# Two of four weight sums added by VectorE into buffers of their own, and row numbers with a buffer per expert

## The chip, the cores and the metric

One core of a Trainium2 chip runs the whole program. The metric is the time of one execution on the device, in microseconds.

## The reference

Attention over 8 batches, 8 heads, 576 tokens and 64 columns a head, each token looking back over 128 tokens with a linear bias; its result is 4608 rows of 512 columns. Each row then goes to one of eight experts:

```
expert_idx = argmax(xn @ en.T / tau, axis=1)      # one expert for each row
for e in range(8):
    mask = expert_idx == e
    h = np.maximum(x[mask] @ w1[e], 0.0)          # w1[e]: 512 x 1024
    out[mask] = gate_w[mask, None] * (h @ w2[e])  # w2[e]: 1024 x 512
```

## The kernel before

Attention takes the first 260 us or so, and its last steps sort the rows by expert into a table in HBM, each with its row number and its gate. Then come the experts, one after the other, in the order of `TURNS` (a list of ranks, the fullest expert being rank 0, of which attention has already done a part). Every value is kept as a pair of fp16 tiles, a high and a low part, and a product is three matmuls. For each expert there is a hidden layer (`x @ w1`, TensorE, with the ReLU and the splitting into two parts done by ScalarE and VectorE) and an output layer (`h @ w2`, in tiles of 128 rows, each 24 matmuls of 512 columns; ScalarE scales the result by the gate, GpSimd stores the rows with an indirect DMA by their numbers).

**The hidden layer with seven products.** The first two experts use a plain product. For the six others (`PLAIN = 2`) `w1` is cut into four quarters of 256 x 512 and the rows of `x` into halves, and seven products stand for eight. The seven weights are three quarters, named `11`, `21` and `22`, and four sums: `t1` and `t3`, each of two quarters, `t2`, which is `t3` and one quarter more, and `t4`, which is `t2` and another one. In the list `SEVEN` the products follow in the order `11`, `t2`, `t3`, `t1`, `21`, `t4`, `22`, four times over (`ft`), and write the banks `ps7a` to `ps7d`. Between them `combine` (lines 1540 on) works: ScalarE copies `ps7a` to `s` (line 1546), VectorE adds it to `ps7b` and that to `ps7d` (both `u`, line 1543), and `ps7b` is then rewritten from `ps7c` and `u` (line 1544), which the last product into `ps7c` needs.

**The weights of the sums.** `fetch_quarter` (line 1417) loads a quarter of fp32 by SyncE's queue; five are loaded. `gather` (line 1421) lets an accumulating DMA of GpSimd's queue add another quarter onto a tile that has landed (line 1425). `t1` and `t3` are made so. For `t2` and `t4` the tile of `t3` is used again: once it has been split, a DMA adds a quarter onto it, that is split as `t2`, a DMA adds another one, and that is split as `t4`. `split` (line 1427) makes the fp16 pair: ScalarE the high part (line 1437), VectorE the low part (line 1435). The pair's tile holds all seven weights and there is one (`w1s=1`), so no split of an expert runs before the seven products of the expert ahead of it are done: the splits lie in that expert's output layer. `fetch` and `part` do the same for `w2` (lines 1409, 1489 and 1487), whose tiles of fp32 come from the same pool of `WSTG = 8` buffers as the quarters.

**Row numbers.** `row_info` (line 1380) is VectorE's: it converts `info`, the loaded numbers and gates of an expert (line 1395), compares the places with the count (1396), writes the row numbers `ids` (1397) and the gates `gs` (1398). It runs for the next expert while the current one starts. `ids` and `gs` have two buffers each. `put` stores a tile of 128 rows to the places in `ids`.

**The order of the work.** `Plan` is a scheduler in the kernel's own text. Each job has an engine, an estimated time, jobs it comes after, buffers it takes (`makes`) and uses, and a due time; for loads also an estimate of the landing (`land`) and of the time on the shared DMA path (`moves`). It lays the jobs out in time by these estimates, picks by due time, lets `fill` jobs give way to others that become ready soon, and emits them; every engine then runs its own list in that order, and waits at each instruction until its inputs are there. `row_info` is planned after the stores of the expert two turns back (`rows=2`), with no landing time for a store.

Of the kernel before, what the change touches and what calls it, by code (L numbers as in the profile page):

```python
# [15 lines left out]
F32 = mybir.dt.float32  # L16
I32 = mybir.dt.int32
AF = mybir.ActivationFunctionType
ALU = mybir.AluOpType
# [4 lines left out]
P = 128  # L24
# [16 lines left out]
GUARD = 32  # L41
PLAIN = 2
XSUM = "DVE"
PIECES = {
    "11": (0, (0, 0), 1),
    "22": (2, (1, 1), 1),
    "21": (1, (1, 0), 1),
    "t3": (5, (1, 1), 1),
    "t1": (3, (0, 1), -1),
}  # L50
CHAINS = {"t1": [(0, 0)], "t3": [(0, 1)], "t2": [(0, 0)], "t4": [(1, 0)]}
WIDTHS = {"t2": (4, -1), "t4": (6, 1)}
SEVEN = [
    ("a", 0, ("x", 0, 0)),
    ("b", 4, ("s", 2, 0)),
# [13 lines left out]
ORDER = -1e9  # L69
# [139 lines left out]
def kernel(  # L209
# [11 lines left out]
    nc = tc.nc  # L221
    B, H, S, D = q.shape
    NTOK, DM = out.shape
    E, _, F = moe_w1.shape
# [1085 lines left out]
    def moe(mctx):  # L1310
        def pool(nm, n):
            return mctx.enter_context(tc.tile_pool(name=nm, bufs=n))

        xt, yp, st, ht, wT, wS, zp = (
            pool(*a)
            for a in (("xt", 2), ("yp", 3), ("wstage", WSTG), ("ht", 1), ("wthird", 1), ("wseven", 1), ("xsum", 1))
        )
        MB = (MAXCAP + P - 1) // P
        MH = max(SLOTS[s] for s in TURNS[PLAIN:]) // 2
        HF = F // 2  # L1320
# [58 lines left out]

        def row_info(s):  # L1380
            (nb, hb), b0, info = blocks(s), first_row(s) // P, state[s]["info"]
            ids = yp.tile([P, MB], I32, tag="ids", name=f"ids_{s}", bufs=2)
            gs = yp.tile([P, MB], F32, tag="gs", name=f"gs_{s}", bufs=2)
            jobs = [(slice(0, P), slice(b0, nb), ids[:, b0:nb], gs[:, b0:nb])]
            if hb:
                pr, pk = tail_rows(s), packs.setdefault(PACKED[s][0], {})
                if not pk:
                    pk["ids"] = yp.tile([P, 1], I32, tag="ids2", name=f"ids2_{s}", bufs=2)
                    pk["gs"] = yp.tile([P, 1], F32, tag="gs2", name=f"gs2_{s}", bufs=2)
                jobs.append((pr, slice(nb, nb + 1), pk["ids"][pr], pk["gs"][pr]))  # L1390
# [23 lines left out]
        def quarter_of(s, q, e):  # L1414
            return moe_w1[ds(e, 1), q[0] * DM // 2 : (q[0] + 1) * DM // 2, q[1] * HF : (q[1] + 1) * HF].rearrange("o (c p) f -> p (o c) f", p=P)

        def fetch_quarter(s, what):
            ws[s, what] = x = st.tile([P, 2, HF], F32, tag="ws", name=f"ws_{what}_{s}")
            nc.sync.dma_start(x, quarter_of(s, PIECES[what][1], state[s]["e"]))

        def gather(s, what, q):

            if what in ("t2", "t4"):
                ws[s, what] = ws[s, "t3"]
            nc.gpsimd.dma_start(ws[s, what], quarter_of(s, q, state[s]["ep"]), accum_op=ALU.add)  # L1425

        def split(s, what, lo):

            if "w1" not in state[s]:
                state[s]["w1"] = [wS.tile([P, 7, 2, HF], F16, tag=f"w1{n}", name=f"w1{n}_{s}") for n in "hl"]  # L1430
            at, sign = WIDTHS[what] if what in WIDTHS else PIECES[what][::2]
            x = ws[s, what].rearrange("p a f -> p (a f)")
            hi, lo_ = (a[:, at].rearrange("p a f -> p (a f)") for a in state[s]["w1"])
            if lo:
                nc.vector.scalar_tensor_tensor(lo_, x, sign * SW, hi, op0=ALU.mult, op1=ALU.subtract)  # L1435
            else:
                nc.scalar.activation(hi, x, AF.Copy, scale=sign * SW)  # L1437
# [200 lines left out]
        def before(name):  # L1638
            return [(name, ORDER)]
# [6 lines left out]
            pe_last = name  # L1646

        starts = {}
        t = 0.0
        for p, s in enumerate(TURNS):  # L1650
            starts[s] = t
# [3 lines left out]
        for p, s in enumerate(TURNS):  # L1655
# [17 lines left out]
            if p:  # L1673
                last_ = TURNS[p - 1]
                m = starts[last_] + 24 * (0.42 * SLOTS[last_] + 5) * (3.5 if p > PLAIN else 4 if p > 1 else 2)
                sp_last = None
                seven_ = p >= PLAIN
                first_gets = [("q", what) for what in ("t3", "t1", "22", "21", "11")] if seven_ else [(1, c) for c in range(4)]
                for n, (w_, c) in enumerate(first_gets + [(2, c) for c in range(4)]):
                    d = (lead - 3000 if w_ != 2 else m) + 1500 * n  # L1680
                    if w_ == "q":
                        name, key, emit = f"getq_{s}_{c}", ("ws", s, c), lambda a=(s, c): fetch_quarter(*a)
                    else:
                        name, key, emit = f"get{w_}_{s}_{c}", ("ws", p, s, w_, c), lambda a=(p, s, w_, c): fetch(*a)
                    J(
                        name, "SP", 640, emit, land=1800, moves=1400, makes=[("ws", key)], due=d,
                        after=before(f"expert{s}") + before(f"rows{last_}") + (before(sp_last) if sp_last else []),
                    )
                    sp_last = name
                if seven_:  # L1690
                    J(f"epool{s}", "POOL", 600, lambda s=s: expert_on_pool(s), after=[f"expert{s}"], due=lead - 2000)
                    wt = {"t2": "t3", "t4": "t3"}
                    dep = {"t1": "getq_{}_t1", "t3": "getq_{}_t3", "t2": "slo_{}_t3", "t4": "slo_{}_t2"}
                    for what in ("t3", "t1", "t2", "t4"):
                        q, late = CHAINS[what][0], what in wt
                        J(
                            f"add_{s}_{what}", "POOL", 1000, lambda a=(s, what, q): gather(*a), land=2200, moves=1400,
                            after=[f"epool{s}", dep[what].format(s)], uses=[("ws", s, wt.get(what, what))], due=lead + 1000 if not late else m + 1000,
                        )
                    made = None  # L1700
                    for n, what in enumerate(("t3", "t1", "11", "t2", "21", "22", "t4")):
                        key = ("ws", s, wt.get(what, what))
                        src = [f"add_{s}_{what}"] if what[0] == "t" else [f"getq_{s}_{what}"]
                        d = m + 1800 * n
                        J(
                            f"shi_{s}_{what}", "ACT", 1020, lambda a=(s, what): split(*a, False), uses=[key],
                            after=src + ([made] if made else []), makes=[] if made else [("w1s", ("w", 1, s))], due=d, fill=True,
                        )
                        made = made or f"shi_{s}_t3"
                        J(  # L1710
                            f"slo_{s}_{what}", "DVE", 1190, lambda a=(s, what): split(*a, True), uses=[key], port=True,
                            after=[f"shi_{s}_{what}"], due=d + 500, fill=True,
                        )
# [22 lines left out]
                for w_, c in [(w_, c) for w_ in ((2,) if p >= PLAIN else (1, 2)) for c in range(4)]:  # L1736
                    a = (p, s, w_, c)
                    key = ("ws",) + a
                    d = m + 1500 * c + 6000 if p >= PLAIN else (lead if w_ == 1 else t0) + 2000 * c + 1000
                    J(  # L1740
                        f"whi{w_}_{s}_{c}", "ACT", 1020, lambda a=a: part(*a, False), uses=[key],
                        after=[f"get{w_}_{s}_{c}"] + ([(f"whi{w_}_{s}_{c-1}", ORDER)] if c else []),
                        makes=[(f"w2{p % 3}" if w_ == 2 else "w1s", ("w", w_, s))] if c == 0 else [], due=d + 3000, fill=True,
                    )
                    J(
                        f"wlo{w_}_{s}_{c}", "DVE", 1190, lambda a=a: part(*a, True), uses=[key], port=p >= PLAIN,
                        after=[f"whi{w_}_{s}_{c}"], due=d + 3500, fill=True,
                    )
# [203 lines left out]
```

## Time and profile before

| what | us |
|---|---|
| median of 3 runs | 676.33 |
| lowest and highest | 673.91, 681.24 |
| the profiled execution, whole | 673.03 |
| its span, first to last instruction | 671.3 |
| TensorE busy in the span | 604.5 |
| VectorE busy | 481.7 |
| ScalarE busy | 381.1 |
| GpSimd busy | 308.8 |

A profile's names: PE is TensorE (PEld its weight loads), DVE VectorE, ACT ScalarE, POOL GpSimd, SP SyncE, which issues most of the loads. An instruction is named by its line, its engine and what it writes and reads (`out<-in`). Idle time in front of an instruction is put down to what came last before it could start, the releaser; "issue" is time in which the profile shows nothing that was waited for. A named releaser can be an engine that was itself held up. PEclk is the clock that TensorE was granted, as a share of 2.4 GHz; 0.5 is its lower level, 1.2 GHz.

### The profile page before, as it was taken

The numbers are of one execution on the slowest core, as the hardware profiler recorded it, in microseconds if no ns is written. First come the engines' busy times: TensorE is split into PE (matmuls) and PEld (weight loads), VectorE is DVE, ScalarE is ACT, GpSimd is POOL, SyncE is SP. The second block draws the span as 40 slices with busy tenths as digits, with TensorE's granted clock in tenths as the row PEclk, the third lists the DMA queues.
The fourth block names the chain that finished last, engine by engine and source line by source line (L and its number), as shares of the span: only waits on it lengthen the run. The fifth ranks groups of instructions, "written<-read, shape, count | busy, mean of one in ns | idle before, by whom it ended". The sixth has DMA issues, their size and how long they took to land. (4 is left out here: it accounts for less than half of the span.)

```text
span 671.3 us, 17414 instructions
## 1 busy us (share of the span) xinstructions
PE 604.5 (90%) x6613; PEld 405.5 (60%) x6613; DVE 481.7 (72%) x1220; ACT 381.1 (57%) x867; POOL 308.8 (46%) x479
## 2 busy tenths in 40 slices
PE   7999998998988899898997995797798799699996
PEld 5787776777766664555645743554564564464764
DVE  4988998899998996343953992693595588395580
ACT  5999897998878852331704552461371364354321
POOL 7878688888978886030032032033126214104101
PEclk9999999999999999898997999799699699899999
DMA  9999999999999965999388389059659559514101
GB/s 186 207 189 193 192 189 211 190 212 229 183 222 252 170 168 186 289 253 218 72 241 217 114 194 329 11 102 297 136 113 303 113 123 323 127 32 95 44 16 49
DMA packets 224821, 117.25 MB, mean 175 GB/s; under 512 B 196309, under 2 KB 196309, under 8 KB 224736
## 3 DMA queue, kind: packets, MB, share of 16 engines
q1 hardware_dynamic: 212368, 84.62, 58.7%
q0 software_dynamic: 12368, 31.50, 18.7%
q8 instruction: 53, 0.87, 0.6%
q14 instruction: 32, 0.26, 0.1%
HBM read 77.65 MB, written 19.70 MB: 145 GB/s over the span
## 5 line engine op out<-in xcount | busy, mean ns | idle before, releaser
L1425 POOL DMA_DIRECT2D ws_t<-moe_w_dram x24 | 30.8, 1392 | 197.6 <-DVE w1l L1435 176.5
L1532 PEld LDWEIGHTS <-w1h 128*128 128x128 f16 x672 | 68.9, 103 | 57.4 <-issue 36.8
L1609 PE MATMUL ps<-w2h,hh 128*128 128x512 f16 (+1 forms) x264 | 98.4, 373 | 0.0
L1609 PE MATMUL ps<-w2h,hl 128*128 128x512 f16 (+1 forms) x264 | 98.4, 373 | 0.0
L1609 PE MATMUL ps<-w2l,hh 128*128 128x512 f16 (+1 forms) x264 | 98.4, 373 | 0.0
L447 POOL DMA_INDIRECT out_dram<-y,ids x32 | 53.5, 1670 | 86.6 <-ACT y L1621 58.7
L695 ACT ACTIVATE pe<-sc,nm 128x128 f32<-128x128 f32 x288 | 84.9, 387 | 8.0 <-DVE nm L688 3.2
L1609 PEld LDWEIGHTS <-hh 128*128 128x128 f16 x528 | 51.5, 98 | 57.9 <-issue 0.8
L1532 PE MATMUL ps7c<-S,w1h 128*128 128x264 f16 (+4 forms) x192 | 39.1, 298 | 26.5 <-DVE ps7b L1544 26.5
L547 DVE SCALAR_TENSOR_TENSOR pq<-ptp,pq 128x512 f16<-128x512 f32 x72 | 53.1, 737 | 13.6 <-ACT pq L544 13.6
L544 ACT ACTIVATE pq<-ptp 128x512 f16<-128x512 f32 x72 | 55.4, 769 | 10.5 <-PE ptp L703 7.7
L703 PE MATMUL ptp<-ident,pe 128*128 128x128 f32 x288 | 48.0, 284 | 13.1 <-DVE pq L547 5.5
L671 PE MATMUL sc<-kh,qh 64*64 64x192 f32 (+3 forms) x1280 | 58.2, 289 | 0.0
L1435 DVE SCALAR_TENSOR_TENSOR w1l<-ws_t,w1h 128x1024 f16<-128x1024 f32 x24 | 29.3, 1222 | 39.9 <-ACT w1h L1437 39.9
L688 DVE TENSOR_REDUCE nm<-sc 128x2 f32<-128x256 f32 x144 | 55.7, 410 | 0.8 <-PE sc L671 0.7
L1437 ACT ACTIVATE w1h<-ws_t 128x1024 f16<-128x1024 f32 x24 | 25.1, 1049 | 53.0 <-DMA ws_t<-moe_w_dram 53.0
L671 PEld LDWEIGHTS sc<-kh,qh 64*64 64x64 f32 (+1 forms) x1280 | 45.0, 139 | 8.7 <-issue 3.6
L1567 ACT ACTIVATE hh<-ps7b 128x264 f16<-128x264 f32 (+4 forms) x24 | 11.6, 485 | 66.9 <-DVE ps7b L1544 66.9
L1532 PE MATMUL ps7a<-xT,w1h 128*128 128x264 f16 (+4 forms) x192 | 40.3, 301 | 8.2 <-ACT s L1546 8.2
L1512 PE MATMUL ps<-xT,w1h 128*128 128x288 f16 (+2 forms) x192 | 42.7, 317 | 4.8 <-DVE hl L1573 2.8
L820 POOL TENSOR_TENSOR gx<-xf,gx 128x512 f16<-128x512 f32 x36 | 42.2, 1173 | 8.5 <-DVE gx L809 7.4
L703 PEld LDWEIGHTS ptp<-ident,pe 128*128 128x128 f32 x288 | 31.6, 141 | 23.4 <-ACT pe L695 13.8
(265 smaller groups left out, 1703.8 us busy)
## 6 DMA issues: line engine op xcount, KB each, us to landing
ws<-moe_w_dram SPq DMA_DIRECT2D x50, 512.0 KB, 6.0
ws_t<-moe_w_dram POOLq DMA_DIRECT2D x24, 512.0 KB, 6.8
ldk<-k_dram SPq DMA_DIRECT2D x32, 256.0 KB, 4.8
ldq<-q_dram SPq DMA_DIRECT2D x32, 256.0 KB, 5.0
ldv<-v_dram SPq DMA_DIRECT2D x32, 256.0 KB, 5.3
ws_t<-moe_w_dram SPq DMA_DIRECT2D x12, 512.0 KB, 5.9
stg<-moe_w_dram SPq DMA_DIRECT2D x16, 256.0 KB, 4.5
ldk<-k_dram SPq DMA_DIRECT2D x8, 128.0 KB
```

Of the source, the lines that this page charges most:

```text
L447: ins = nc.gpsimd.indirect_dma_start(out[:, :], bass.IndirectOffsetOnAxis(ap=ids, axis=0), y, None, bounds_check=NTOK - 1, oob_is_err=False)
L544: nc.scalar.activation(hi, ps, AF.Copy, scale=scale)
L547: nc.vector.scalar_tensor_tensor(lo, ps, scale, hi, op0=ALU.mult, op1=ALU.subtract)
L671: nc.tensor.matmul(sc[T, hf, j][o, l, c], qT[T]["h"][rows, hp, o], x["h"][rows, hp, c.start + at : c.stop + at], start=False, stop=True, s ...
L688: nc.vector.tensor_reduce(nm_t[T, hf, j], sc[T, hf, j][:, :, 0:P], axis=AX.X, op=ALU.min)
L695: nc.scalar.activation(pr_t[T, hf][:, 2 * l + j, :], ps[:, l, 0:P], AF.Exp, bias=nm[:, l : l + 1], scale=-1.0)
L703: nc.tensor.transpose(pt[:, i, :], pe[:, i, :], ident)
L820: nc.gpsimd.tensor_tensor(xx[:, DM : 2 * DM], xf_t[T], xx[:, 0:DM], op=ALU.subtract)
L1425: nc.gpsimd.dma_start(ws[s, what], quarter_of(s, q, state[s]["ep"]), accum_op=ALU.add)
L1512: nc.tensor.matmul(ps[:, :w], a[:, kt, fs], xx[:, b + kt, c0 : c0 + w], start=(n == 0), stop=(n == len(jobs) - 1))
L1532: nc.tensor.matmul(ps, a[:, idx, c, fs], b[:, c, :], start=(n in OPENS and m == 0), stop=(m == len(jobs) - 1), skip_group_check=True)
L1609: nc.tensor.matmul(ps, x[:, ft, a * P : (a + 1) * P], w[:, ft, c], start=(n == 0), stop=(n == len(jobs) - 1))
```

## The change

`gather` keeps the accumulating DMA for `t1` and `t3` alone. `t2` and `t4` get tiles of their own from the pool of eight, and VectorE adds `t3 + 11` and `t2 + 21` into them, as jobs that may fill and that are planned after the quarter `22` was issued. The quarters are loaded in the order `t3`, `11`, `t1`, `21`, `22`, and split in the order `11`, `t3`, `t1`, `t2`, `21`, `22`, `t4`. The first load of `w2` is issued, in the plan's order, after the sum `t4`; the splits of `w2` have later due times; the list of loads on SyncE is now tied together across experts (`sp_last` is set once). The estimates of the two accumulating DMAs that stay are longer. `ids` and `gs` have eight buffers.

```diff
-            ids = yp.tile([P, MB], I32, tag="ids", name=f"ids_{s}", bufs=2)
-            gs = yp.tile([P, MB], F32, tag="gs", name=f"gs_{s}", bufs=2)
+            ids = yp.tile([P, MB], I32, tag="ids", name=f"ids_{s}", bufs=8)
+            gs = yp.tile([P, MB], F32, tag="gs", name=f"gs_{s}", bufs=8)
...
-        def gather(s, what, q):
-
-            if what in ("t2", "t4"):
-                ws[s, what] = ws[s, "t3"]
-            nc.gpsimd.dma_start(ws[s, what], quarter_of(s, q, state[s]["ep"]), accum_op=ALU.add)
+        def gather(s, what):
+
+            if what in ("t1", "t3"):
+                q = (0, 0) if what == "t1" else (0, 1)
+                nc.gpsimd.dma_start(ws[s, what], quarter_of(s, q, state[s]["ep"]), accum_op=ALU.add)
+            else:
+                ws[s, what] = x = st.tile([P, 2, HF], F32, tag="ws", name=f"ws_{what}_{s}")
+                a, b = ("t3", "11") if what == "t2" else ("t2", "21")
+                (nc.gpsimd if TSUM == "POOL" else nc.vector).tensor_tensor(x, ws[s, a], ws[s, b], op=ALU.add)
...
+        sp_last = None
...
-                sp_last = None
                 seven_ = p >= PLAIN
-                first_gets = [("q", what) for what in ("t3", "t1", "22", "21", "11")] if seven_ else [(1, c) for c in range(4)]
+                first_gets = [("q", what) for what in ("t3", "11", "t1", "21", "22")] if seven_ else [(1, c) for c in range(4)]
...
+                    back_ = [f"sum_{s}_t4"] if (w_, c) == (2, 0) and seven_ else []
...
-                        after=before(f"expert{s}") + before(f"rows{last_}") + (before(sp_last) if sp_last else []),
+                        after=before(f"expert{s}") + before(f"rows{last_}") + (before(sp_last) if sp_last else []) + [(b_, ORDER) for b_ in back_],
...
-                    for what in ("t3", "t1", "t2", "t4"):
-                        q, late = CHAINS[what][0], what in wt
+                    for n, what in enumerate(("t3", "t1")):
                         J(
-                            f"add_{s}_{what}", "POOL", 1000, lambda a=(s, what, q): gather(*a), land=2200, moves=1400,
-                            after=[f"epool{s}", dep[what].format(s)], uses=[("ws", s, wt.get(what, what))], due=lead + 1000 if not late else m + 1000,
+                            f"sum_{s}_{what}", "POOL", 1300, lambda a=(s, what): gather(*a), land=4000, moves=2800,
+                            after=[f"epool{s}", f"getq_{s}_{what}"], uses=[("ws", s, what)], due=lead + 1000 + 1500 * n,
+                        )
+                    for what, a, b in (("t2", "t3", "11"), ("t4", "t2", "21")):
+                        ns = 2300 if TSUM == "POOL" else 1150
+                        J(
+                            f"sum_{s}_{what}", TSUM, ns, lambda a=(s, what): gather(*a), **(dict(lock=(ns,)) if TSUM == "POOL" else dict(port=True, fill=True)),
+                            after=[(f"sum_{s}_{a}" if a[0] == "t" else f"getq_{s}_{a}"), f"getq_{s}_{b}"] + before(f"getq_{s}_22"),
+                            uses=[("ws", s, k) for k in (a, b, what)], makes=[("ws", ("ws", s, what))], due=lead + 9000,
                         )
...
-                    for n, what in enumerate(("t3", "t1", "11", "t2", "21", "22", "t4")):
+                    for n, what in enumerate(("11", "t3", "t1", "t2", "21", "22", "t4")):
...
-                    d = m + 1500 * c + 6000 if p >= PLAIN else (lead if w_ == 1 else t0) + 2000 * c + 1000
+                    d = t0 + 2500 * c if p >= PLAIN else (lead if w_ == 1 else t0) + 2000 * c + 1000
```

## Rows read from the trace of the kernel before

**Rows 1.** Page: span; busy us of each engine, its share and instructions.

```profile
span 671.3 us, 17414 instructions
...
PE 604.5 (90%) x6613; PEld 405.5 (60%) x6613; DVE 481.7 (72%) x1220; ACT 381.1 (57%) x867; POOL 308.8 (46%) x479
```

**Rows 2.** TensorE's waits from 300 us: what for; us in total, times, longest.

```profile
PE ps7c L1532 <- DVE ps7b L1544: 26.5, 5, 10.7
PE ps7a L1532 <- ACT s L1546: 8.2, 2, 4.1
PE ps L1512 <- DVE hl L1573: 2.8, 1, 2.8
```

**Rows 3.** Timeline of VectorE, 400 to 427 us: start, us, instruction [idle before].

```profile
421.71 0.17 DVE L1397 SCALAR_TENSOR_TENSOR ids<-got,far 128x4 int32<-128x4 f32 x1 [10.72 <-DMA out_dram<-y,ids]
...
422.52 0.47 DVE L1544 SCALAR_TENSOR_TENSOR ps7b<-ps7c,u 128x288 f32<-128x288 f32 x1
```

**Rows 4.** Line 1397, VectorE: its waits, us and times.

```profile
  DMA out_dram<-y,ids: 20.7, 3
  issue: 7.9, 2
```

**Rows 5.** Timeline of GpSimd, 400 to 427 us.

```profile
408.36 2.63 POOL L1425 DMA_DIRECT2D ws_t<-moe_w_dram  x2
411.30 1.08 POOL L447 DMA_INDIRECT out_dram<-y,ids  x1 [0.30 <-issue]
```

**Rows 6.** Timeline of ScalarE, 450 to 480 us.

```profile
467.03 1.06 ACT L1437 ACTIVATE w1h<-ws_t 128x1024 f16<-128x1024 f32 x1 [9.29 <-DMA ws_t<-moe_w_dram]
...
468.56 0.38 ACT L1546 ACTIVATE s<-ps7a 128x264 f32<-128x264 f32 x1
```

**Rows 7.** Line 1425, accumulating loads: who waited; us to landing.

```profile
  ACT w1h L1437: 53.0, 10
...
DMA to landing us min/median/max: 5.8/6.8/10.8
```

**Rows 8.** Stretches behind five gaps: length, engines' busy us, PEclk, DMA share, GB/s.

```profile
363.50:369.50 6.00, 6.00 (x30) 3.98 (x30) 3.01 (x8) 1.66 (x4) 0.00 (x0) 0.55 0.74 132
423.00:427.50 4.50, 4.46 (x21) 2.89 (x21) 2.17 (x6) 2.32 (x5) 0.00 (x0) 0.56 0.00 0
468.00:481.50 13.50, 8.58 (x39) 5.63 (x39) 6.44 (x20) 3.88 (x9) 3.91 (x3) 0.50 0.67 149
522.00:533.50 11.50, 7.85 (x40) 5.22 (x39) 4.33 (x15) 2.94 (x6) 3.20 (x3) 0.55 0.77 160
581.00:584.00 3.00, 2.67 (x11) 1.53 (x11) 2.38 (x6) 1.43 (x3) 0.00 (x0) 0.51 0.00 0
```

**Rows 9.** VectorE from 300 us by line and shape: busy us, mean ns.

```profile
L1435 DVE SCALAR_TENSOR_TENSOR w1l<-ws_t,w1h 128x1024 f16<-128x1024 f32 x24 | 29.3, 1222 | 39.9 <-ACT w1h L1437 39.9
...
L1457 DVE TENSOR_TENSOR z<-z 128x624 f32<-128x624 f32 x4 | 3.2, 808 | 0.1
```

**Rows 10.** The first stretch below, line 1487 (VectorE) alone: length, busy us.

```profile
363.50:382.00 18.50, 3.65 (x3) 0.85 0.43 101
```

**Rows 11.** A hidden layer, then two output layers; columns as rows 8.

```profile
363.50:382.00 18.50, 18.50 (x134) 14.11 (x134) 14.38 (x33) 6.83 (x17) 0.00 (x0) 0.85 0.43 101
382.00:408.00 26.00, 26.00 (x194) 11.81 (x193) 20.84 (x25) 15.90 (x22) 7.28 (x6) 1.00 0.89 233
440.00:465.00 25.00, 24.92 (x132) 12.73 (x131) 18.00 (x25) 11.29 (x17) 10.60 (x7) 1.00 0.84 217
```

**Rows 12.** Timeline of SyncE's queue, 500 to 545 us.

```profile
506.02 29.58 SPq L1409 DMA_DIRECT2D ws<-moe_w_dram  x3
```

**Rows 13.** Timeline of GpSimd, 480 to 512 us.

```profile
498.14 1.19 POOL L1425 DMA_DIRECT2D ws_t<-moe_w_dram  x1 [25.29 <-DVE w1l L1435]
500.94 9.89 POOL L447 DMA_INDIRECT out_dram<-y,ids  x1 [1.61 <-ACT y L1621]
511.14 1.32 POOL L447 DMA_INDIRECT out_dram<-y,ids  x1 [0.30 <-issue]
```

More of the change, by code (lines that the diff above doesn't have):

```diff
@@ L43 @@
 XSUM = "DVE"
[L44 to L52, printed above, removed]
+TSUM = "DVE"
+PIECES = {"11": (0, 1), "21": (1, 1), "22": (2, 1), "t1": (3, -1), "t2": (4, -1), "t3": (5, 1), "t4": (6, 1)}
 SEVEN = [
@@ L1417, in fetch_quarter @@
         def fetch_quarter(s, what):
+            q = {"t1": (0, 1), "t3": (1, 1)}.get(what) or (int(what[0]) - 1, int(what[1]) - 1)
             ws[s, what] = x = st.tile([P, 2, HF], F32, tag="ws", name=f"ws_{what}_{s}")
-            nc.sync.dma_start(x, quarter_of(s, PIECES[what][1], state[s]["e"]))
-        def gather(s, what, q):
-            if what in ("t2", "t4"):
-                ws[s, what] = ws[s, "t3"]
-            nc.gpsimd.dma_start(ws[s, what], quarter_of(s, q, state[s]["ep"]), accum_op=ALU.add)
+            nc.sync.dma_start(x, quarter_of(s, q, state[s]["e"]))
+        def gather(s, what):
[6 more added lines that the diff above has]
+                (nc.gpsimd if TSUM == "POOL" else nc.vector).tensor_tensor(x, ws[s, a], ws[s, b], op=ALU.add)
         def split(s, what, lo):
@@ L1430, in split @@
                 state[s]["w1"] = [wS.tile([P, 7, 2, HF], F16, tag=f"w1{n}", name=f"w1{n}_{s}") for n in "hl"]
-            at, sign = WIDTHS[what] if what in WIDTHS else PIECES[what][::2]
+            at, sign = PIECES[what]
             x = ws[s, what].rearrange("p a f -> p (a f)")
@@ L1691, in moe @@
                     J(f"epool{s}", "POOL", 600, lambda s=s: expert_on_pool(s), after=[f"expert{s}"], due=lead - 2000)
-                    wt = {"t2": "t3", "t4": "t3"}
-                    dep = {"t1": "getq_{}_t1", "t3": "getq_{}_t3", "t2": "slo_{}_t3", "t4": "slo_{}_t2"}
-                    for what in ("t3", "t1", "t2", "t4"):
-                        q, late = CHAINS[what][0], what in wt
-                        J(
-                            f"add_{s}_{what}", "POOL", 1000, lambda a=(s, what, q): gather(*a), land=2200, moves=1400,
-                            after=[f"epool{s}", dep[what].format(s)], uses=[("ws", s, wt.get(what, what))], due=lead + 1000 if not late else m + 1000,
+                    for n, what in enumerate(("t3", "t1")):
+                        J(
+                            f"sum_{s}_{what}", "POOL", 1300, lambda a=(s, what): gather(*a), land=4000, moves=2800,
[7 more added lines that the diff above has]
+                            uses=[("ws", s, k) for k in (a, b, what)], makes=[("ws", ("ws", s, what))], due=lead + 9000,
                         )
                     made = None
-                    for n, what in enumerate(("t3", "t1", "11", "t2", "21", "22", "t4")):
-                        key = ("ws", s, wt.get(what, what))
-                        src = [f"add_{s}_{what}"] if what[0] == "t" else [f"getq_{s}_{what}"]
-                        d = m + 1800 * n
+                    for n, what in enumerate(("11", "t3", "t1", "t2", "21", "22", "t4")):
+                        key = ("ws", s, what)
+                        src = [f"sum_{s}_{what}"] if what[0] == "t" else [f"getq_{s}_{what}"]
+                        d = m + 1300 * n
                         J(
@@ L1708, in moe @@
                         )
-                        made = made or f"shi_{s}_t3"
+                        made = made or f"shi_{s}_{what}"
                         J(
```

## The prediction

> **What bounds the kernel now.** I read the page first: TensorE is busy for 604.5 of 671.3 us [rows 1], so about 67 us of the span hold no matmul, and a faster DMA or a lighter engine is worth only what it gives back there. The second view, TensorE's waits from 300 us on, says where: 26.5 us in five waits of the product `ps7c` for VectorE's `ps7b`, 8.2 us in two waits of `ps7a` for ScalarE's `s`, and 2.8 us elsewhere [rows 2]. That is 37.5 us, all at the start of an expert's hidden layer or, the 2.8, within one.
>
> A releaser named there is only the last link, so the third view is VectorE's order of work in one of these gaps. `ps7b` at 422.52 does not wait for TensorE: it stands in the queue behind `ids`, which waited 10.72 us and ran at 421.71 [rows 3]. The instruction is line 1397 in `row_info`, and its line's waits add up to 28.6 us in five, 20.7 of them put down to the stores of `out` that read `ids` [rows 4]. The other two are called "issue"; they stand at the same instruction, between the same neighbours, in two of the five gaps, so I count them as the same wait. `ids` has two buffers, so the row numbers of the next expert overwrite those of the expert that has just ended, and must wait until its last store has landed. In the gap shown, that store was issued at 411.30, behind two accumulating loads that GpSimd issued from 408.36 [rows 5]. The conversion of `info` one line earlier had already run, so the rows were there: the buffer is what is late.
>
> The two waits for `s` are another chain. ScalarE stood 9.29 us at the high part of a weight sum until its accumulating DMA had landed, and the copy `s`, which TensorE needs, is queued behind it, at 468.56 [rows 6]. That sum is `t4`. It cannot begin before `t3` was split, overwritten by `t2`, landed and split again. Such a DMA lands 5.8 to 10.8 us after issue, 6.8 in the median, and ScalarE waited 53.0 us for them in all [rows 7].
>
> A gap costs more than its length. After each, TensorE goes on at its lower level, 1.2 GHz: the mean granted clock is 0.50 to 0.56 in the stretches behind the gaps [rows 8]. At full clock, busy time times (1 - clock) would be saved: 6.00 x 0.45 = 2.70, 4.46 x 0.44 = 1.96, 8.58 x 0.50 = 4.29, 7.85 x 0.45 = 3.53, 2.67 x 0.49 = 1.31; in sum 13.8 us.
>
> **The change, part by part.**
>
> *A buffer of row numbers per expert.* Eight buffers for eight experts: nothing is overwritten, and the 28.6 us of waiting at line 1397 go. `far` and `got` keep two buffers, but only VectorE touches them. The planner's ring of two stays, so `row_info` stands where it stood in VectorE's order. What is late next is `ps7b` itself: in the gap shown its time from the release of `ids` is 422.52 - 421.71 = 0.81 us to its start and about 0.5 us to run, 1.3 us. Taken from 410.99, where the wait began (421.71 - 10.72), it would end near 412.3; TensorE went idle at 423.04 - 10.65 = 412.39. So the gap closes. I take all 26.5 us [rows 2]; the lower end, if `ps7b` is half a microsecond late at five places, is 24.
>
> *`t2` and `t4` by VectorE.* Twelve of the 24 accumulating DMAs go (two each for six experts), with their issue on GpSimd. In their place stand twelve additions of 128x1024 fp32. No row shows that one exactly: the low part of a split reads two tiles of the same size and takes 1.222 us, and the addition of two fp32 tiles of 624 columns takes 0.808, which scales to 1.33 at 1024 [rows 9]. I take 1.22, so 2.4 us per expert, 14.6 us in all, with 16 as the upper end. Their operands are a landed quarter and the sum before it, and their results have buffers of their own, so they need not wait for the splits; they can run a stage ahead. `t4` is then ready when its split is due, ScalarE has nothing to wait for before `s`, and the 8.2 us go. The lower end is zero: the stage start would wait for something else.
>
> *Where the 2.4 us lie.* In the first hidden layer shown VectorE is busy 14.38 of 18.5 us, with three splits of the second weight, 3.65 us, among it [rows 10, 11]; without them 10.7. TensorE loses 2.7 us of that stretch to the clock, so at full clock it is 15.8 long. 14.4 + 2.4 = 16.8 does not fit into 15.8 unless one split moves on. In the output layers VectorE is busy 20.84 of 26.0 and 18.00 of 25.0 us [rows 11], so 5 to 7 us are free there, and the splits move into it; `fill` jobs yield to work that TensorE waits for. If a sum runs just ahead of a combination, it costs up to its 1.2 us. I charge 1 us for each of five stages, 5 us, between 0 (all hidden) and 12 (both sums on the path in each of five stages).
>
> *Order and buffers.* Seven quarter tiles and four of the second weight now pass through eight buffers, eleven instead of nine. Tiles 1 to 3 of the second weight take the buffers of `t3`, `11` and `t1` of the same expert and wait for their splits; behind them on SyncE's queue wait the transposed rows of a later expert and, since the loads are tied together across experts, the next expert's quarters. I cost it at nothing: before, SyncE already spends 29.58 us on three such loads [rows 12], most of it waiting for buffers, and TensorE has no gap at the output layer that uses them [rows 2]. The second weight is needed only after the next hidden layer, some 40 us later. The later due time of its splits only ranks them behind those of the first weight. Twelve fewer DMAs also leave less in the queue that the stores share.
>
> *The sum.* 26.5 + 8.2 + 13.8 = 48.5 us go; 671.3 - 48.5 = 622.8; plus 5 is a span of 627.8 us. The profiled execution took 673.03, 1.7 more than its span, which gives 629.5. The median of the runs shown, 676.33, is 3.3 above that execution; between the two readings, 629.5 and 632.8, I say 631.
>
> *A stretched store.* At 500.94 one store takes GpSimd 9.89 us, in a stretch in which VectorE is working without a break on instructions with two SBUF inputs; the next takes 1.32, and an accumulating load in the same dense stretch 1.19 [rows 13]. The store reads a list of rows in SBUF, the load does not. The Trainium skill, SBUF — State Buffer, section "Who interferes with whom", says that a VectorE instruction with two SBUF inputs contends with a GpSimd instruction that reads SBUF; the trace agrees in kind. By that rule the new sums lengthen stores, and the result is a rival below.
>
> **The rivals.**
>
> *The sums wait for the first DMA.* `t2` needs `t3`, still an accumulating DMA, and VectorE takes its work in order. If the sum's place in the order comes before the landing, everything behind it waits, as now behind `ids`. The plan allows 6.8 us from issue to landing, the median; the longest is 10.8 [rows 7]. 4 us at each of five stages, and some 2 us of low clock behind each, are 30 us: 622.8 + 30 is a span of 652.8, and a time of 655 to 658. Against it: the loads lie a stage ahead, and their issue need not wait for splits.
>
> *Stores held by the sums.* Two sums per expert hold a store by 2.4 us; through six experts 14.6 us if it came through to TensorE: 645. Against it: what the store held for 9.89 us kept back was the accumulating load of `t4` queued behind it, which goes, and the wait at `ids`, which goes too; `y` has three buffers.
>
> *No change.* The wait at line 1397 is replaced by another one at the same place, for instance for `info`: about 676.
>
> *Slower.* The eleven tiles starve each other: a second weight arrives after its hidden layer has ended, and TensorE stands at the output layer. It decides once a load comes over 40 us after the buffer's due release, against 10.8 us for the longest landing of a part of the weights that stopped an engine here [rows 7]. To be slower by over 1% it must give back 48.5 and 6.8, 55 us, 9 us per expert: about 684.
>
> **How the numbers follow.** Forecast 0.68 (own range 620 to 641: all hidden and the low run, to both sums exposed), waiting sums 0.15, held stores 0.06, no change 0.05, slower 0.06. The range 620 to 652 holds the forecast, the held stores and about a third of the waiting sums, some 8 in 10. About 1% is what a measurement of this kernel can tell from no change; faster by more is 0.68 + 0.15 + 0.06 = 0.89, within it 0.05, slower 0.06.
>
> **What would show it.** Right: no wait at line 1397; TensorE's waits for `ps7b` and `s` under 5 us together; the granted clock at full level through the hidden layers; a new line of twelve additions near 1.22 us; twelve accumulating loads. Wrong: VectorE idle ahead of the additions until `ws` lands (first rival), idle ahead of `got` until `info` lands (no change), TensorE idle at `ps` of the output layer (slower), ScalarE idle ahead of `y` (held stores).

## The result

| what | before | after |
|---|---|---|
| median of four runs each, us | 676.8 | 647.57 |
| lowest and highest, us | 673.91, 681.24 | 641.54, 649.06 |
| the profiled execution, whole, us | 673.03 | 649.06 |
| its span, us | 671.3 | 647.4 |

The ratio is 0.9546, with a 95% interval of 0.9466 to 0.9626. The kernel is faster and the time lies in the range, but 16.6 us above the forecast of 631 and above the likeliest case's own range, which ended at 641. So a part of the sum was wrong, or something was added that the sum lacks. That it still lies in the range is in part luck: the range reached up to 652 for the held stores and the waiting sums, and most of what came on top is another wait, which the prediction put at nothing.

**The page of after**: span, TensorE's line, and the granted clock in forty slices (tenths of full speed). These answer [rows 1].

```profile
span 647.4 us, 17377 instructions
...
PE 590.3 (91%) x6613; PEld 399.7 (62%) x6613; DVE 495.5 (77%) x1232; ACT 381.9 (59%) x867; POOL 287.7 (44%) x467
...
PEclk9999999999999999999669999999989999999999
```

VectorE has twelve instructions more and is busy 13.8 us longer, against 14.6 predicted. TensorE has the same matmuls as before, yet is busy 14.2 us less: more of them ran at the full clock. Two places stay below it, slices 20 and 21 (from 307 us) and slice 30.

**TensorE's waits in after**, from 280 us on (what for; us in total, times, longest), answer [rows 2].

```profile
PE ps L1510 <- DVE hl L1571: 20.0, 1, 20.0
PE ps7d L1530 <- DVE u L1541: 5.7, 2, 4.7
PE ps7c L1530 <- DVE ps7b L1542: 0.6, 1, 0.6
```

The 26.5 us for `ps7b` are 0.6, and the 8.2 us for `s` are gone. In their place stand 5.7 us for `u`, and the wait for `hl`, 2.8 us before, is 20.0.

**After by line**: first VectorE's additions, then ScalarE's high parts of the sums (times, busy us, mean ns, idle before them), which answer [rows 6]; last, from the view of line 1419, who waited for the accumulating loads and their landing, which answers [rows 7].

```profile
L1423 DVE TENSOR_TENSOR ws_t<-ws_t,ws 128x1024 f32<-128x1024 f32 x12 | 14.7, 1221 | 11.7 <-DMA ws_t<-moe_w_dram 11.6
...
L1435 ACT ACTIVATE w1h<-ws_t 128x1024 f16<-128x1024 f32 x24 | 24.4, 1045 | 0.0
...
  DVE ws_t L1423: 11.6, 4
...
DMA to landing us min/median/max: 8.4/9.8/24.6
```

An addition takes 1.22 us, as the sum had it. ScalarE's 53.0 us of waiting for accumulating loads are gone; VectorE waits 11.6 us for them instead, ahead of four additions. The twelve loads that stay land later than before: 9.8 us in the median against 6.8, and 24.6 at the longest against 10.8.

**Where the 23.9 us of span came from.** TensorE's waits fell from 37.5 to 26.3 us, 11.2 less. The low clock behind the gaps cost 13.8 us in the five stretches of [rows 8], and 3.72 x 0.43 = 1.6 in a sixth that the prediction had not counted; in after it costs 3.55 x 0.50 = 1.8 and 7.31 x 0.28 = 2.0. That is 15.4 against 3.8, 11.6 less. Together 22.8 of the 23.9 us. The stretches, of before and then of after (length; TensorE, weight loads, VectorE, ScalarE, GpSimd busy; granted clock; DMA share; GB/s):

```profile
314.00:318.00 4.00, 3.72 (x15) 2.08 (x15) 4.00 (x6) 1.41 (x2) 0.00 (x0) 0.57 0.95 358
```

```profile
330.00:334.00 4.00, 3.55 (x13) 1.93 (x13) 4.00 (x7) 0.00 (x0) 0.00 (x0) 0.50 0.57 148
464.00:476.00 12.00, 7.31 (x47) 5.22 (x45) 6.65 (x20) 3.21 (x6) 1.24 (x3) 0.72 0.48 110
```

Had the first wait stayed at 2.8 us, the span would be 647.4 - 17.2 = 630.2, some 2 us from the forecast span of 627.8. So the question is what that one wait is.

**The 20 us wait.** It stands at the third expert, the first with seven products, at the end of the hidden layer ahead of it. First the rows of after: SyncE's queue, GpSimd, VectorE and TensorE (start, us, instruction, idle before).

```profile
292.21 0.97 SPq L1402 DMA_DIRECT2D ws<-moe_w_dram  x2
293.46 0.37 SPq L1413 DMA_DIRECT2D ws_t<-moe_w_dram  x1
294.10 0.37 SPq L1413 DMA_DIRECT2D ws<-moe_w_dram  x1
294.72 0.48 SPq L1413 DMA_DIRECT2D ws_t<-moe_w_dram  x1
295.40 16.08 SPq L1349 DMA_TRANSPOSE xT<-xs  x1
...
300.11 1.32 POOL L1419 DMA_DIRECT2D ws_t<-moe_w_dram  x1 [25.68 <-ACT hh L1573]
...
303.19 1.23 POOL L1419 DMA_DIRECT2D ws_t<-moe_w_dram  x1 [0.37 <-issue]
...
325.59 1.29 DVE L1449 TENSOR_TENSOR z<-xT 128x1088 f32<-128x1088 f16 x1 [24.87 <-DMA xT<-xs]
328.72 0.17 DVE L1388 CAST got<-info 128x4 f32<-128x4 int32 x1 [1.83 <-DMA info<-xs]
...
329.87 0.96 DVE L1571 SCALAR_TENSOR_TENSOR hl<-ps,hh 128x352 f16<-128x352 f32 x2
...
330.45 0.72 PE L1510 MATMUL ps<-xT,w1h 128*128 128x336 f16 x2 [20.03 <-DVE hl L1571]
```

The same place before: the quarters `t3` and `t1` and the transposing load on SyncE's queue, both accumulating loads on GpSimd, VectorE's first use of `info`, which follows the transposing load on the queue, and its `z`.

```profile
289.01 1.01 SPq L1419 DMA_DIRECT2D ws_t<-moe_w_dram  x2
...
295.07 14.73 SPq L1356 DMA_TRANSPOSE xT<-xs  x1
...
293.70 2.57 POOL L1425 DMA_DIRECT2D ws_t<-moe_w_dram  x2 [20.55 <-DMA ws_t<-moe_w_dram]
...
312.42 0.17 DVE L1395 CAST got<-info 128x4 f32<-128x4 int32 x1 [11.83 <-DMA info<-xs]
...
314.14 1.28 DVE L1451 TENSOR_TENSOR z<-xT 128x1088 f32<-128x1088 f16 x1
```

SyncE loads the expert's rows of `x` transposed into `xT`. Before, both accumulating loads were issued 1.4 us ahead of it; 17.4 us after its issue VectorE had `info`, and `z` ran after 19.1 without a wait. In after SyncE's list is tied together across experts, the last two loads of the second weight come first, `t3` is loaded 4.5 us later, and the accumulating loads are issued 4.7 and 7.8 us behind the transposing load, beside it. VectorE's `z`, the first use of `xT`, starts 30.2 us after its issue. VectorE takes its work in order: `hl` of the expert before, which has nothing to do with `xT`, is queued behind `z` and the late row numbers, starts at 329.87, and TensorE waits for it. The low clock behind it is a consequence.

**The smaller wait, 4.7 us.** GpSimd, then VectorE, then TensorE in after:

```profile
452.90 6.97 POOL L440 DMA_INDIRECT out_dram<-y,ids  x1 [3.42 <-ACT y L1619]
459.85 2.59 POOL L1419 DMA_DIRECT2D ws_t<-moe_w_dram  x2
...
466.51 1.23 DVE L1423 TENSOR_TENSOR ws_t<-ws_t,ws 128x1024 f32<-128x1024 f32 x1 [4.53 <-DMA ws_t<-moe_w_dram]
467.65 0.43 DVE L1541 TENSOR_TENSOR u<-ps7b,s 128x264 f32<-128x264 f32 x1
...
469.63 0.60 PE L1530 MATMUL ps7d<-xT,w1h 128*128 128x264 f16 x2 [4.69 <-DVE u L1541]
```

A store took GpSimd 6.97 us in place of the 1.1 of its neighbours; the two accumulating loads queued behind it landed late; the addition that makes `t2` stood at the head of VectorE's list until then, and `u`, which TensorE needed, behind it. This is the first rival (waiting sums), brought about by a store of the kind of [rows 13]. None of the new sums ran during that store: VectorE was at splits and at `z`. The other wait for `u`, 1.0 us at 376.56, lies in the third expert's hidden layer: the two additions for the fourth, which waited 5.84 us for their load, ran there at 372.47, ahead of `u`.

### The profile page after: what moved, and what is told of

Read it like the earlier page. It is cut to its first block, busy times and chain, and to the rows that moved or that the text cites. A ratio compares the mean times of both kernels' runs of the same rounds, so it can differ in the third digit from the quotient of the medians.

```text
span 647.4 us, 17377 instructions
## 1 busy us (share of the span) xinstructions
PE 590.3 (91%) x6613; PEld 399.7 (62%) x6613; DVE 495.5 (77%) x1232; ACT 381.9 (59%) x867; POOL 287.7 (44%) x467
## 5 line engine op out<-in xcount | busy, mean ns | idle before, releaser
L440 POOL DMA_INDIRECT out_dram<-y,ids x32 | 49.0, 1531 | 233.4 <-ACT y L1619 166.9
L1530 PEld LDWEIGHTS <-w1h 128*128 128x128 f16 x672 | 65.7, 98 | 23.9 <-issue 6.8
L540 DVE SCALAR_TENSOR_TENSOR pq<-ptp,pq 128x512 f16<-128x512 f32 x72 | 53.2, 739 | 14.2 <-ACT pq L537 13.9
L1510 PE MATMUL ps<-xT,w1h 128*128 128x288 f16 (+2 forms) x192 | 41.4, 310 | 21.4 <-DVE hl L1571 20.0
L1619 ACT ACTIVATE y<-ps,gs 128x512 f32<-128x512 f32 (+1 forms) x28 | 18.9, 676 | 67.4 <-PE ps L1607 67.3
L764 PE MATMUL av<-vh,mp 128*128 128x65 f16 (+1 forms) x512 | 43.0, 195 | 2.0 <-issue 1.2
L1607 PEld LDWEIGHTS <-hl 128*128 128x128 f16 x264 | 25.8, 98 | 29.4
L613 POOL TENSOR_TENSOR vo<-ldv,vh 128x512 f16<-128x512 f32 x36 | 40.7, 1134 | 6.7 <-ACT vh L605 6.1
L928 POOL DMA_INDIRECT xs<-gx,di x36 | 37.1, 1032 | 10.5 <-issue 5.1
L674 DVE COPY_PREDICATED sc<-mask_full,sc 128x256 f32<-128x256 int32 x96 | 38.3, 420 | 3.7 <-PE sc L664 3.7
```

The lines of the kernel that those rows point to most:

```text
L440: ins = nc.gpsimd.indirect_dma_start(out[:, :], bass.IndirectOffsetOnAxis(ap=ids, axis=0), y, None, bounds_check=NTOK - 1, oob_is_err=False)
L540: nc.vector.scalar_tensor_tensor(lo, ps, scale, hi, op0=ALU.mult, op1=ALU.subtract)
L764: nc.tensor.matmul(o_, a_, b_, start=False, stop=(n == last), skip_group_check=True)
L1510: nc.tensor.matmul(ps[:, :w], a[:, kt, fs], xx[:, b + kt, c0 : c0 + w], start=(n == 0), stop=(n == len(jobs) - 1))
L1530: nc.tensor.matmul(ps, a[:, idx, c, fs], b[:, c, :], start=(n in OPENS and m == 0), stop=(m == len(jobs) - 1), skip_group_check=True)
L1607: nc.tensor.matmul(ps, x[:, ft, a * P : (a + 1) * P], w[:, ft, c], start=(n == 0), stop=(n == len(jobs) - 1))
```

## The experiments

Three theories stood for the missing 16.6 us: that the two halves of the change were mis-sized (each was run alone); that loads of GpSimd beside the transposing load make the 20 us wait; and, as rivals to that, that the plain loads just ahead of it on SyncE's queue make it, or VectorE's order there whatever the loads do. The runs were made on other chips than the comparison above, where before took 683.3 (the first four), 683.5 (the next four) and 675.5 us (the last two), so ratios to before are compared, each with its 95% interval.

### Buffers of row numbers alone

```diff
# the kernel before
-            ids = yp.tile([P, MB], I32, tag="ids", name=f"ids_{s}", bufs=2)
-            gs = yp.tile([P, MB], F32, tag="gs", name=f"gs_{s}", bufs=2)
+            ids = yp.tile([P, MB], I32, tag="ids", name=f"ids_{s}", bufs=8)
+            gs = yp.tile([P, MB], F32, tag="gs", name=f"gs_{s}", bufs=8)
```

> The kernel before with eight buffers for the row numbers and gates, and nothing else changed: one half of the change alone. Theory (the waits of row_info for the last store were five of the gaps, 26.5 us, with about 9 of the 13.8 us of low clock behind them): no wait at the line of ids, TensorE's waits for ps7b near 0, its 8.2 us for s and 2.8 us of the first gap stay, 641 us against 676. Rival (the waits only move: the next thing in line, the sums t4 or the rows, takes their place): TensorE's waits stay above 25 us in all and the time is 655 or more.

Measured: 0.9495 [0.9434, 0.9556], 648.26 us, as expected (641 of 676 is 0.948). TensorE's main waits in this kernel:

```profile
PE ps7a L1532 <- ACT s L1546: 8.5, 2, 4.3
PE ps L1512 <- DVE hl L1573: 3.1, 1, 3.1
PE ps7c L1532 <- DVE ps7b L1544: 1.4, 3, 0.7
```

Two changed numbers give as much as the whole change (0.9546). The waits for `ps7b` fall from 26.5 to 1.4 us, the two for `s` stay at 8.5, and `hl` stays near 3.

### The sums alone

```diff
# the kernel after
-            ids = yp.tile([P, MB], I32, tag="ids", name=f"ids_{s}", bufs=8)
-            gs = yp.tile([P, MB], F32, tag="gs", name=f"gs_{s}", bufs=8)
+            ids = yp.tile([P, MB], I32, tag="ids", name=f"ids_{s}", bufs=2)
+            gs = yp.tile([P, MB], F32, tag="gs", name=f"gs_{s}", bufs=2)
```

> The changed kernel with two buffers for row numbers and gates, as before: the other half alone. Theory: TensorE's two waits for s are gone, the waits at ids stay but are shorter, some 3.5 us each, since fewer accumulating loads stand ahead of the store; the 20 us gap ahead of the first seven-product expert, which the changed order of loads makes, stays: about 668 to 674 us, no change to speak of. Rival (the gap of 20 us comes from the row buffers): the gap is near 3 us and the time is 652 or less.

Measured: 0.978 [0.971, 0.985], 667.41 us, somewhat better than expected. TensorE's waits:

```profile
PE ps L1510 <- DVE hl L1571: 16.5, 1, 16.5
PE ps7d L1530 <- DVE u L1541: 9.9, 4, 6.3
PE ps7c L1530 <- DVE ps7b L1542: 8.3, 2, 5.9
```

The long wait for `hl` comes with this half of the change. The halves do not add: 5.05% and 2.2% alone, 4.5% together. In after the half with the buffers adds only 2.4%.

### The third expert's accumulating loads held until its rows have landed

GpSimd copies one column of `xT` first, so its two accumulating loads stand behind the transposing load.

```diff
+                if s == TURNS[PLAIN] and what == "t3":
+                    seen = yp.tile([P, 1], F16, tag="seen", name=f"seen_{s}", bufs=1)
+                    nc.gpsimd.tensor_copy(seen, state[s]["xT"][:, 2 * KT - 1, SLOTS[s] - 1 : SLOTS[s]])
...
-                            after=[f"epool{s}", f"getq_{s}_{what}"], ...
+                            after=[f"epool{s}", f"getq_{s}_{what}"] + ([f"rows{s}"] if p == PLAIN else []), ...
```

> The changed kernel, in which GpSimd copies one column of the transposed rows of the third expert (the first with seven products) before it issues the two accumulating loads of that expert, so that these no longer run beside the transposing load. SyncE's queue is as in the changed kernel. Theory (the 20 us gap at 310 us is the transposing load, slowed by the two accumulating loads beside it): the transposed rows land near 310 us instead of 325, the gap is 5 us or less, 628 to 632 us. Rival (the rows are late because SyncE issues four loads of 512 KB right ahead of them): the gap stays at 15 us or more, 643 to 648 us.

Measured: 0.9306 [0.9251, 0.9361], 637.39 us. SyncE's queue, GpSimd, VectorE, and TensorE's waits:

```profile
301.71 10.42 SPq L1349 DMA_TRANSPOSE xT<-xs  x1
...
318.15 1.31 POOL L1421 COPY seen<-xT 128x1 f16<-128x1 f16 x1 [8.62 <-DMA xT<-xs]
319.40 2.56 POOL L1422 DMA_DIRECT2D ws_t<-moe_w_dram  x2
...
318.12 1.29 DVE L1452 TENSOR_TENSOR z<-xT 128x1088 f32<-128x1088 f16 x1 [10.97 <-DMA xT<-xs]
...
PE ps7d L1533 <- DVE u L1544: 5.9, 2, 4.1
PE ps L1513 <- DVE hl L1574: 3.0, 1, 3.0
```

With no load of GpSimd's beside it (two of its stores are, as in after), the transposing load takes 16.4 us to its first use in place of 30.2, though the same five loads of SyncE's queue stand ahead of it. The wait for `hl` is 3.0 us. With the sums alone, which ran on this chip too, it took 27.2 us, so the chip is not the cause. VectorE's list is the same up to `hl`, so its order whatever the loads do is not the cause either; and the plain loads ahead do not make the 20 us, though the next run shows that they have a share. Two stretches of 16 us within the transposing load's time, in after from 16.6 us behind its issue and here from 0.3:

```profile
312.00:328.00 16.00, 0.00 (x0) 0.00 (x0) 1.29 (x1) 0.00 (x0) 0.00 (x0) 0.55 1.20 164
```

```profile
302.00:318.00 16.00, 16.00 (x105) 10.08 (x103) 3.02 (x3) 4.44 (x7) 3.06 (x4) 1.00 1.15 261
```

In after the DMA engines are as busy as here (1.20 against 1.15), and move 164 GB/s in place of 261. From issue to first use it is 174 GB/s (1.27) against 266 (1.15). The lowest place in after lies right behind GpSimd's two loads: from 305 to 312 us 76 GB/s are moved. No run shows why.

### The third expert's rows ahead of its quarters

```diff
-... + [(b_, ORDER) for b_ in back_],
+... + [(b_, ORDER) for b_ in back_] + (before(f"rows{s}") if p == PLAIN and w_ == "q" else []),
```

> The changed kernel, in which SyncE issues the transposing load of the third expert's rows ahead of the five quarters of that expert. The accumulating loads come after the quarters and so later still. By the theory (accumulating loads beside the transposing load slow it): the rows land between 308 and 318 us, since it starts some 3 us earlier and the accumulating loads reach only its end; gap 0 to 8 us, 628 to 636 us. By the rival (plain loads ahead of it): the gap vanishes as well, so this run alone doesn't tell the two apart, but with the run in which GpSimd waits it does. If neither holds (the transposing load is slow by itself at this place), the gap stays over 12 us, 640 us or more.

Measured: 0.929 [0.9231, 0.935], 635.75 us. The transposing load was issued at 303.31 behind two loads only and GpSimd's came at 316.37 and 320.60; `z` started at 312.72, 9.4 us after the issue. Against the 16.4 of the run before, that is some 7 us for the three quarters that stood ahead of it there, one execution each. TensorE's wait for `hl` at this place is gone; 5.7 us for `u` stay. Either way of parting the loads comes out near the forecast ratio, 631 / 676.3 = 0.933.

### After once more, and plain loads in place of accumulating ones

After itself, run beside the next three:

> The changed kernel once more, on the chip of the runs beside it, so that its ratio to the kernel before can be set against theirs. Expected: ratio 0.945 to 0.965, and again one gap of 15 to 20 us ahead of the third expert.

Measured: 0.9544 [0.9491, 0.9597], 653.91 us, with waits of 18.2 us for `hl` and 5.6 for `u`; 29.4 us from the issue of the transposing load to `z`.

In the other kernel the two loads of GpSimd for the third expert overwrite the tile and do not add, so the first quarters of `t1` and `t3` of that expert are left out.

```diff
-                nc.gpsimd.dma_start(ws[s, what], quarter_of(s, q, state[s]["ep"]), accum_op=ALU.add)
+                if s == TURNS[PLAIN]:
+                    nc.gpsimd.dma_start(ws[s, what], quarter_of(s, q, state[s]["ep"]))
+                else:
+                    nc.gpsimd.dma_start(ws[s, what], quarter_of(s, q, state[s]["ep"]), accum_op=ALU.add)
```

> The changed kernel, in which the two loads that GpSimd issues for the third expert are plain and don't add: the first quarter of the two sums of this expert is left out. Queue, place and bytes are the same. If adding is what slows the transposing load beside it (a reading and a writing of SBUF for every packet), the rows land some 16 to 20 us after issue and the gap is under 6 us, near 0.93 of the kernel before. If any two loads of 512 KB on GpSimd's queue do it, they land after 27 us or more and the gap stays over 12 us, 0.945 to 0.96.

Measured: 0.9439 [0.9378, 0.95], 646.8 us; 24.1 us to `z`, and a wait of 11.3 us for `hl`, between the two outcomes that were expected. Loads of GpSimd's queue that add nothing thus still lengthen the transposing load, by 7.7 us (24.1 - 16.4) between one execution of each kernel, on two chips. What the adding costs on top I can't give: against after again it is 5.3 us (29.4 - 24.1), but a kernel shown below (the later sum without the rows first), with accumulating loads in the same places, needed only 23.4. The intervals of the two ratios overlap a little. That share stays open.

### The first of VectorE's sums planned later

The kernel with the rows first, and `t2` planned 6 us after its accumulating load is due.

```diff
-                            after=[(f"sum_{s}_{a}" if a[0] == "t" else f"getq_{s}_{a}"), f"getq_{s}_{b}"] + before(f"getq_{s}_22"),
+                            after=[(f"sum_{s}_{a}", 6000 if a == "t3" else 0), f"getq_{s}_{b}"] + before(f"getq_{s}_22"),
```

> The kernel with the rows of the third expert first, and t2 planned 6 us later than its accumulating load's planned landing. Theory (the sum's place in VectorE's order comes before the landing, the first rival of the prediction): VectorE's waits at the sums, some 12 to 15 us, fall to under 4, TensorE's 5.7 us of waits for u fall under 2, and with the clock behind them 5 to 8 us are gained on the kernel with the rows first (0.929 of before): 0.918 to 0.924. Rival (the waits at the sums are hidden but for one, or come back elsewhere): 0.926 to 0.932.

Measured: 0.9132 [0.9082, 0.9182], 625.7 us, better than expected. All of TensorE's waits from 280 us on:

```profile
PE ps L1510 <- DMA xT<-xs: 1.4, 1, 1.4
PE ps L1607 <- DVE hl L1571: 0.6, 1, 0.6
```

The additions wait 2.2 us for their loads in place of 15.4 with the rows first alone, and the mean granted clock is 0.997 (0.977 in after). This version beats both kernels: 57.8 us below before on the same chip. The prediction's three terms and the wait of 2.8 us are 51.3 of them; the other 6 or so I did not trace.

The same later sum without the rows first:

> The changed kernel with t2 planned 6 us later, and the loads of the third expert in the changed kernel's order (not the rows first). If the two losses are separate, the gap of 15 to 20 us ahead of the third expert stays and TensorE's waits for u vanish: 0.936 to 0.944 of the kernel before, against 0.954 for the changed one and 0.913 with both mended. If the later sums also move the loads enough to close the gap, 0.92 or less.

Measured: 0.9423 [0.9376, 0.9469], 634.85 us, with a shorter gap than the 15 to 20 us expected. One wait of TensorE is left:

```profile
PE ps L1510 <- DVE hl L1571: 12.6, 1, 12.6
```

The two losses are separate: the waits for `u` are gone here and the wait for `hl` is not. But that wait is 7.4 us shorter than in after, so the step from 0.954 to 0.942 is not the price of the later sum alone. Here the transposing load needed 23.4 us to `z`, with the accumulating loads 5.0 and 7.7 us behind it, so that delay is not the same from kernel to kernel that has this order: 30.2 in after, 29.4 in after again, 27.2 with the sums alone, 23.4 here.

### No accumulating loads at all

With the rows first, four quarters are loaded, GpSimd adds `t3` and `t1`, VectorE `t2` and `t4`.

```diff
-                first_gets = [("q", what) for what in ("t3", "11", "t1", "21", "22")] if seven_ else [(1, c) for c in range(4)]
+                first_gets = [("q", what) for what in ("22", "t1", "11", "21")] if seven_ else [(1, c) for c in range(4)]
...
+            a, b, eng = {"t3": ("22", "t1", nc.gpsimd), "t1": ("t1", "11", nc.gpsimd), "t2": ("t3", "11", nc.vector), "t4": ("t2", "21", nc.vector)}[what]
+            x, y = ws[s, a], ws[s, b]
+            if what != "t1":
+                ws[s, what] = st.tile([P, 2, HF], F32, tag="ws", name=f"ws_{what}_{s}")
+            eng.tensor_tensor(ws[s, what], x, y, op=ALU.add)
...
```

> The kernel with the rows of the third expert first, and no accumulating DMA at all: each expert's four quarters are loaded once (four loads instead of seven) and all four sums are added on chip, t3 and t1 by GpSimd, t2 and t4 by VectorE. If the accumulating loads are what is left of the waits, VectorE's waits at the sums vanish and the time is 0.915 to 0.925 of the kernel before. If GpSimd's additions of 1024 columns (2.3 us each by the 1.13 to 1.17 of its 512-column ones) stand in VectorE's way or come late themselves, 0.93 to 0.95.

Measured: 0.9403 [0.9332, 0.9474], 643.11 us, the second of the two outcomes expected and slower than the kernel with the rows first (0.929), though it moves less. TensorE's waits, and GpSimd's additions:

```profile
PE ps7c L1528 <- DVE ps7b L1540: 5.9, 3, 3.3
PE ps7d L1528 <- DVE u L1539: 3.5, 3, 1.9
PE ps7a L1528 <- ACT s L1542: 1.8, 1, 1.8
...
L1421 POOL TENSOR_TENSOR ws_t<-ws_t,ws 128x1024 f32<-128x1024 f32 x6 | 16.2, 2706 | 0.3
```

GpSimd needs 2.7 us in the mean for what VectorE does in 1.22, and small waits return in the hidden layers. Which of them goes back to GpSimd I did not separate.

### The buffers once the rest is mended

The kernel with rows first and the later sum, but `ids` and `gs` with two buffers again.

> The best kernel so far (rows of the third expert first, t2 planned 6 us later) with two buffers for row numbers and gates instead of eight. It prices the buffers once everything else is mended. Theory (the waits for the last store remain, but no accumulating load stands ahead of it in the queue so that they are shorter, 2 to 4 us at each of five experts, of which TensorE feels the larger part, and the clock behind them): 0.93 to 0.945 of the kernel before. Rival (with later sums the stores land in time): 0.92 or less.

Measured: 0.9473 [0.9413, 0.9533], 639.89 us, just above the range expected and 3.7% above the same kernel with eight (0.9473 / 0.9132). From the view of its line 1390, the idle time before `ids`, and the largest of TensorE's waits:

```profile
  DMA out_dram<-y,ids: 19.4, 5
...
PE ps7c L1530 <- DVE ps7b L1542: 14.7, 3, 6.3
```

So the sums do not make the buffers needless, and the wait that they take away comes back at its old place.

## Why the prediction was right and where it failed

- **The buffers of row numbers: right.** Line 1390, the old 1397, has no idle time before it in after; the 26.5 us of [rows 2] became 0.6, and 1.4 with this edit alone. The 28.6 us of [rows 4] were one cause, the two waits called "issue" too: all five went.
- **`t4` off the path: right.** The 8.2 us for `s` are gone with the sums and stay without them (8.5).
- **The clock: right.** The stretches of [rows 8] gave back what they were charged, where no new gap took their place.
- **The sums' price and their cover: right, and most of the 5 us charged too many.** 1.22 us each; TensorE felt their own time only in the third expert's hidden layer, in waits of 1.0 and 0.6 us. In the output layers VectorE became nearly full and TensorE stayed so, as these stretches of two of them in after show:

```profile
440.00:462.00 22.00, 22.00 (x109) 10.44 (x107) 21.69 (x28) 14.77 (x20) 10.16 (x4) 1.00 0.93 289
492.00:510.00 18.00, 18.00 (x93) 8.82 (x91) 17.70 (x19) 11.24 (x16) 7.33 (x8) 1.00 1.01 319
```

  [rows 11] had 5 to 7 us free there. It was splits that moved in, as the prediction had it: line 1485, the second weight, takes 3.49 us in each of the two, against 0.85 in the last stretch of [rows 11]. The sums are in neither; eight of the twelve ran in hidden layers, in the room so made, and four at the end of an output layer. The Trainium skill, VectorE: DVE Perf Modes, section "The TRN2 errata — SBUF-src ops pay a fixed extra latency per instruction", gives (N + 151) / 0.96 ns for such an addition, measured there at N = 512 and 2048; that makes an estimate of 1224 ns at N = 1024. The trace agrees (1221 in the mean).
- **Order and buffers "at nothing": the step that failed.** It looked at SyncE's list for buffers that a load waits for and for weights that come late, and found slack of 40 us. It did not ask what each moved load would then run beside. Tying the list put the third expert's `t3` behind two loads of the second weight, its accumulating load with it, and both accumulating loads into the transposing load of the same expert. Price: 17.2 us more of wait; the low clock behind it costs 1.8 us, about as before (1.6). Parting them again gives the ratio from 0.954 to 0.929 or 0.931, 16 to 17 us of 683. That loads beside the transposing load are the cause is shown by two kernels that mend it in different ways; that the tie is what moved them (with `11` now loaded ahead of `t1`) is read from the two orders and was not tried by itself.
- **The first rival: partly true, at two stages of five, 4.7 and 1.0 us of wait.** The prediction counted on loads that lie a stage ahead. At 452.90 a stretched store of the kind of [rows 13] stood ahead of them on GpSimd, 6.97 us, and the plan gives a landing 6.8 us (4.0 and 2.8 on the shared path) where the median is now 9.8. The cost is 5.7 us and 2.0 of clock; with the rows first, planning `t2` later takes the ratio from 0.929 to 0.913, and no wait for `u` is left. "Held stores" was thus no case of its own: no sum ran during that store, and it mattered only through the accumulating loads that remained queued behind it.
- **No change, and slower: neither.** From 300 us on `got` waits for `info` once, 1.83 us, behind the late transposing load, and TensorE never waits at an output layer for `w2`.
- **The number.** Forecast span 627.8, measured 647.4, 630.2 without the growth of the one wait. That the rest comes within 3 us is in part luck: of the 5 us charged for the sums little was paid, and the first rival's 5.7 of wait and 2.0 of clock, which the sum did not hold, took their place.

## What to carry to other kernels

When a change reorders a queue, go through each transfer that moves and write down what will be in flight beside it; a slow kind of transfer (here the transposing load) is the one to protect, by a dependency or by issuing it first. When an engine that works in order gets an instruction that waits for a transfer, plan it by the late landings, not by the median, since everything behind it waits as well. And before a larger rebuild, try its smallest part alone: here two numbers gave as much as the whole change, and the rebuild paid only after its two new waits were found.

## What the runs showed of the hardware

- A transposing load of one expert's rows, from its issue to the first use: 9.1 to 9.7 us in the four kernels with two plain loads just ahead of it, 16.4 with five, 24.1 with five and two plain loads of GpSimd's queue issued beside it, 23.4 to 30.2 with five and two accumulating ones, in four executions. Before, with the accumulating ones issued 1.4 us ahead of it, the rows had landed by 19.1.
- The accumulating loads suffer too: the two beside the transposing load in after needed over 24 us to landing, against 10.8 at the longest before [rows 7]. The Trainium skill, DMA: Bandwidth & Descriptors, section "SWDGE vs HWDGE vs iDMA", says that GpSimd's and SyncE's transfers feed different queues within each DMA engine, which takes turns between them. The traces agree in that each of the two slows the other; that the whole moves less, 174 against 266 GB/s from issue to first use, does not follow from taking turns.
- GpSimd adds two tiles of 128x1024 fp32 in 2.7 us in the mean, VectorE in 1.22.
